# Sketched attention and a squared-relu FFN on one core: a shorter prologue, and later batches computed feature-major

## Chip, cores and metric

One core of a Trainium2 chip. The metric is device microseconds (us) of one execution; lower is better. A run is about 1.8 us longer than the span of its profile. With one core, "slow" only marks a run more than 1.5% above the fastest of the same kernel. Ratios use fast runs alone; medians below are of all runs, and where slow runs weigh in them, the fast ones are given too.

## The reference

Four batches, four heads, 1088 tokens, head size 32; then an FFN over all 4352 tokens, 128 wide, 2048 hidden.

```python
def phi(x):                                   # r = 8, so 64 features
    a = np.einsum('rd,bhsd->bhsr', S1, x)
    b = np.einsum('rd,bhsd->bhsr', S2, x)
    return np.einsum('bhsi,bhsj->bhsij', a, b).reshape(*x.shape[:-1], r * r)
q_p, k_p = phi(q), phi(k)
kv  = np.einsum('bhsf,bhsd->bhfd', k_p, v)
z   = np.sum(k_p, axis=2)
num = np.einsum('bhsf,bhfd->bhsd', q_p, kv)
den = np.einsum('bhsf,bhf->bhs', q_p, z)[..., None] + 1e-06
x   = (num / den), heads side by side         # 4352 x 128
g   = np.maximum(x @ w_in, 0.0) ** 2
out = g @ w_out
```

## The kernel before

Every operation is a node of a graph with engines that may run it and a modelled duration; the kernel schedules the graph itself when it is built, by a tuned list of priorities, and emits the instructions in that order. Each engine then works in that fixed order. All four batches use one form of attention, and all loads of batch 0 are on SyncE's queue:

```python
# key sketch: 32 wide, 64 columns                                     L416
nc.tensor.matmul(o[32*g : 32*g+32, :, j-j0, :], kT[i][:, 32*c : 32*c+32],
                 SK.rearrange("p x h r -> p x (h r)"), ...)
# keys times values, with a column of ones for z: 64 wide, 33 columns  L448
nc.tensor.matmul(t[64*(h%2) : 64*(h%2)+64, 33*(h//2) : 33*(h//2)+33],
                 kp[i][:, j, h, :], vp[i][:, h, j, :], ...)
# query sketch, both repeats (ab = 0, 1)                               L495
for ab in range(2): ... nc.tensor.matmul(at(hb[x])[64*y : 64*y+64, c0 : c0+n], SR[32*h : 32*h+32, ab], rhs, ...)
# numerator and denominator, token-major: 32 wide, 66 columns          L539
nc.tensor.matmul(at(nb)[32*cc : 32*cc+32, col(x=x, pr=pr)], qp[i][:, pr, n0 : n0+32], kvz[i][xx%2][:, pr], ...)
# ... normalise on VectorE, transpose back by TensorE (L571), copy into xT, then FFN:
# h = x w_in (L598), r = relu(h) (L607), g = r*r (L614), o += g w_out (L621)
```

Dummy matmuls on zeros (L290) keep TensorE busy before there is work.

## Time and profile before

| | before |
|---|---|
| median of the runs at hand, us | 123.16 (121.44 to 125.42) |
| span of the profile, us | 120.9 |
| busy: PE, DVE, ACT, POOL, us | 107.3, 94.4, 82.0, 25.1 |
| first FFN matmul, last compute, us | 22.36, 116.4 |

The prediction below quotes the windows and the timeline. Two windows it doesn't quote are needed later. Columns: stretch, its length, busy time (and instruction count) of PE, weight loads, VectorE, ScalarE, GpSimd, then granted clock, DMA share, GB/s.

```profile
57.00:74.00 17.00, 16.23 (x345) 9.56 (x347) 14.44 (x30) 12.14 (x20) 0.00 (x0) 1.00 0.11 18
74.00:91.00 17.00, 16.62 (x248) 9.45 (x250) 14.09 (x24) 14.62 (x21) 0.00 (x0) 1.00 0.11 18
```

From 57 us on the DMA engines are nearly idle: all loads are done. The row of the clock that TensorE was granted, in tenths of full speed, shows one dip, after the 2.46 us stop at 16.4. The clock records of the trace have half speed there, so such a stretch is called a half clock below.

```profile
PEclk9999995899999999999999999999999999999999
```

### The profile page before, as it was taken

To read this page: it belongs to the slowest core of one execution; us is meant where nothing else is said; L and a number is where in the kernel's file an instruction comes from. 1 tells how busy PE (TensorE), PEld (TensorE's weight loads), DVE (VectorE), ACT (ScalarE), POOL (GpSimd) and SP (SyncE) were. 2 spreads that over 40 slices of the span, in tenths; PEclk is the share of its full clock that TensorE was granted. 3 is DMA by queue.
4 is the path that set the end of the run, shared out by engine and by line. 5 is a ranking of instruction groups with operands and counts; after the bars stand their busy time and mean duration, and the time that the engine had idled before them with its cause. 6 is when DMAs were issued, how large, how long until landed. Compare 5 with 4: busy or idle time off the path is not lost.

```text
span 120.9 us, 4244 instructions
## 1 busy us (share of the span) xinstructions
PE 107.3 (89%) x1804; PEld 62.6 (52%) x1826; DVE 94.4 (78%) x168; ACT 82.0 (68%) x117; POOL 25.1 (21%) x55
## 2 busy tenths in 40 slices
PE   6999946999998999999999899999999999989530
PEld 2346736455664656556455755664466454645320
DVE  2599442499999999999895899768799987778810
ACT  3153700599769773898679567898966899999300
POOL 5219573726994500000000000000000000000000
PEclk9999995899999999999999999999999999999999
DMA  3985999999972900220000140220001304113051
GB/s 100 253 195 66 173 260 247 185 206 224 316 172 37 253 8 5 43 44 5 0 5 0 24 69 4 45 47 0 0 10 28 54 3 70 22 27 60 3 102 31
DMA packets 22700, 10.26 MB, mean 85 GB/s; under 512 B 19040, under 2 KB 20840, under 8 KB 22680
## 3 DMA queue, kind: packets, MB, share of 16 engines
q0 software_dynamic: 2560, 6.07, 23.3%
q1 hardware_dynamic: 20048, 3.90, 16.3%
q8 instruction: 14, 0.23, 0.9%
q14 instruction: 6, 0.05, 0.1%
q10 hardware_dynamic: 72, 0.01, 0.0%
HBM read 8.80 MB, written 2.23 MB: 91 GB/s over the span
## 4 chain that ended last, share of the span: by engine, by line
PE 59%; DVE 14%; ACT 12%; issue 10%; DVEq 0%; ACTq 0%
PE o L621 15%; PE h L598 13%; ACT r L607 12%; PE h L539 7%; PE h L495 7%; PE o L290 7%; DVE g L614 6%; PE a L448 6%; DVE kp L431 2%; DVE qT L472 2%; PE a L416 2%; PE h L416 1%; DVE qp L514 1%; DVE kT L403 1%; DVE osb L628 1%
## 5 line engine op out<-in xcount | busy, mean ns | idle before, releaser
L607 ACT ACTIVATE r<-h 128x1024 bf16<-128x1024 f32 x67 | 64.1, 1051 | 9.5 <-PE h L598 6.5
L614 DVE TENSOR_TENSOR g<-r 128x1024 bf16<-128x1024 bf16 x68 | 45.2, 687 | 6.0 <-PE o L621 4.5
L621 PE MATMUL o<-g,w_out 128*128 128x512 bf16 (+1 forms) x133 | 36.8, 367 | 2.3 <-DVE osb L628 1.2
L598 PE MATMUL h<-xT,w_in 128*128 128x512 bf16 (+1 forms) x137 | 37.7, 368 | 1.2 <-ACT r L607 0.9
L598 PEld LDWEIGHTS <-w_in 128*128 128x128 bf16 x144 | 15.4, 114 | 15.5 <-issue 2.4
L621 PEld LDWEIGHTS <-w_out 128*128 128x128 bf16 x144 | 12.7, 97 | 14.0 <-issue 3.8
L508 ACT COPY A<-h 128x512 f32<-128x512 f32 (+1 forms) x20 | 9.8, 525 | 6.5 <-PE h L495 6.5
L539 PE MATMUL h<-kvz,qp 128*32 128x66 f32 x576 | 10.6, 228 | 2.8 <-issue 2.5
L514 DVE TENSOR_TENSOR qp<-h,A 128x512 f32<-128x512 f32 x16 | 10.4, 683 | 2.3 <-ACT A L508 2.2
L539 PEld LDWEIGHTS h<-kvz,qp 128*32 128x32 f32 x576 | 9.2, 114 | 5.6 <-issue 3.0
L495 PE MATMUL h<-qT,SR 32*64 32x256 f32 (+1 forms) x320 | 10.8, 355 | 0.0
L290 PE MATMUL o<-wz 128*128 128x512 bf16 x26 | 9.2, 483 | 1.7 <-DVE mk L261 1.2
L448 PEld LDWEIGHTS a<-vp,kp 128*64 128x64 f32 x288 | 9.0, 138 | 2.7 <-issue 2.6
L448 PE MATMUL a<-vp,kp 128*64 128x33 f32 x288 | 9.9, 224 | 0.3
L495 PEld LDWEIGHTS h<-qT,SR 32*64 32x64 f32 x320 | 6.0, 131 | 3.8 <-DVE qT L472 0.4
L372 POOL DMA_DIRECT2D vin<-in_v_dram x12 | 6.6, 555 | 5.4 <-DMA vin<-in_v_dram 1.8
L628 DVE STREAM_TRANSPOSE osb<-o 128x512 f32<-128x512 f32 (+1 forms) x9 | 6.1, 679 | 1.6 <-PE o L621 1.4
L431 DVE TENSOR_TENSOR kp<-a,ka 128x1024 f32<-128x1024 f32 (+1 forms) x5 | 6.6, 1325 | 0.3 <-ACT ka L423 0.3
L388 POOL COPY vp<-vin 128x512 f32<-128x512 f32 x7 | 5.5, 805 | 5.9 <-DMA vin<-in_v_dram 5.3
L290 PEld LDWEIGHTS <-wz 128*128 128x128 bf16 x30 | 3.1, 119 | 5.9 <-issue 3.9
L472 DVE STREAM_TRANSPOSE qT<-qin 128x512 f32<-128x512 f32 (+1 forms) x8 | 5.8, 735 | 0.3 <-DMA qin<-in_q_dram 0.3
L555 DVE TENSOR_TENSOR xs<-h,rec 128x512 bf16<-128x512 f32 x8 | 5.5, 692 | 0.3
(50 smaller groups left out, 62.1 us busy)
## 6 DMA issues: line engine op xcount, KB each, us to landing
kin<-in_k_dram POOLq DMA_DIRECT2D x3, 544.0 KB, 8.8
qin<-in_q_dram POOLq DMA_DIRECT2D x3, 544.0 KB, 6.9
vin<-in_v_dram POOLq DMA_DIRECT2D x12, 128.0 KB, 6.5
out_dram<-osb SPq DMA_DIRECT2D x20, 64.0 KB, 1.9
vin<-in_v_dram SPq DMA_DIRECT2D x8, 64.0 KB, 3.1
kin<-in_k_dram SPq DMA_DIRECT2D x1, 288.0 KB, 4.3
qin<-in_q_dram SPq DMA_DIRECT2D x1, 288.0 KB, 2.7
kin<-in_k_dram SPq DMA_DIRECT2D x1, 256.0 KB, 2.8
```

Source lines behind the costliest of these rows:

```text
L290: nc.tensor.matmul(tiles["o"][0][:, 0:512], wz[:, 0:128], wz, start=True, stop=True)
L431: nc.vector.tensor_tensor(out=kp[i][:, j0:j1].rearrange("p j h (x y) -> p (j h) x y", y=R), in0=bb[:, :, None, :].to_broadcast([128, m, R, ...
L448: nc.tensor.matmul(t[64 * (h % 2) : 64 * (h % 2) + 64, 33 * (h // 2) : 33 * (h // 2) + 33], kp[i][:, j, h, :], vp[i][:, h, j, :], start=(j ...
L472: nc.vector.transpose(qT[i][:, 32 * c0 : 32 * c1], qin[i][:, 32 * c0 : 32 * c1])
L495: nc.tensor.matmul(at(hb[x])[64 * y : 64 * y + 64, c0 : c0 + n], SR[32 * h : 32 * h + 32, ab].rearrange("p x y -> p (x y)"), rhs, start=Tr ...
L508: nc.scalar.copy(at(sA).rearrange("p r e s -> p r (e s)")[:, :, 0:n], src(ab=0))
L514: nc.vector.tensor_tensor(out=qp5[:, u, x], in0=src(ab=1).rearrange("p r (e s) -> p r e s", e=2), in1=at(sA), op=ALU.mult)
L539: nc.tensor.matmul(at(nb)[32 * cc : 32 * cc + 32, col(x=x, pr=pr)], qp[i][:, pr, n0 : n0 + 32], kvz[i][xx % 2][:, pr].rearrange("p y d -> ...
L598: nc.tensor.matmul(at(hb)[:, step * w : step * w + N], w_in[:, 512 * (ct // E) : 512 * (ct // E) + 512].rearrange("p (c e) -> p e c", e=E) ...
L607: nc.scalar.activation(o, view(at(hb)), ACTF.Relu)
L614: nc.vector.tensor_tensor(out=at(gb)[:, 0 : W * N], in0=r, in1=r, op=ALU.mult)
L621: nc.tensor.matmul(at(ob)[:, 0:N], w_out[:, ct, :], at(gb)[:, N * w : N * w + N], start=(ct == 0), stop=(ct == CT - 1))
```

## The change

Three intents. (1) A shorter prologue: k of batch 0 in four pieces over two queues, the two sketch matrices loaded once and spread over the partitions by a matmul, a first FFN tile of 256 tokens. (2) Batches 1 to 3 keep features on the partitions, which makes TensorE's matmuls wider and removes the transposes behind them. (3) The denominator goes into the first repeat of the query, and this has to be repeated over the features: by TensorE for batch 1, by SyncE's DMA queue for batches 2 and 3. The core of the diff (cuts marked; priorities and engine choices were tuned anew):

```diff
-        LQ = {"SP": (0.45, 3.4)} if b == 0 else {"POOL": (0.65, 3.4)}
+        SPQ, ACQ = {"SP": (0.43, 3.4)}, {"ACT": (0.43, 3.4)}
+            o_kh = [[add(f"ldk{b}.{c0}.{y}", ACQ if y else SPQ, ...) for y in range(2)] for c0, c1 in ((0, 16), (16, 34))]
...
+    o_SX = add("SX", {"PE": pe(0.12)}, lambda e: nc.tensor.matmul(
+        at(stb)[:, 0 : 2 * R], repm, ST[:, 0 : 2 * R], start=True, stop=True), ...)
...   # batches 1 to 3: keys times values, 32 wide, 64 columns (L779)
+                        nc.tensor.matmul(at(kvb)[32 * h : 32 * h + 32, 0:F], lhsT, kp[i][0:n, j, h], ...)
...   # z of the keys (L751) folded into two sketches A and U of the query (L810), 272 columns
+        o_Z = add(f"Z{b}", {"PE": pe(0.5)}, f_Z, o_ka, vt(4), alloc=[zb])
+        o_W = add(f"W{b}", {"PE": pe(0.2)}, f_W, [o_ZT] + o_S2B, vt(4.6), alloc=[wb_])
...   # Ad = A / denominator, then spread over the features
+        o_Ad = add(f"Ad{b}", {"DVE": ..., "POOL": ...}, ... out=Ad[i], in0=As[i], in1=Rt[i][:, 0:272], op=ALU.mult ...)
+        if b == 1:
+            ... nc.tensor.matmul(at(rb_[x])[...], EI[32 * g : 32 * g + 32, ...], Ad[i][32 * g : 32 * g + 32, :], ...)
+        for g in range(4 if b > 1 else 0):
+            for pr in range(2):
+                    nc.sync.dma_start(
+                        out=Ar[i][:, pr, 272 * g : 272 * g + 272],
+                        in_=Ad[i][32 * g + 16 * pr : 32 * g + 16 * pr + 16, None, :].to_broadcast([16, 8, 272]))
...   # one repeat left on TensorE (L876), product with the spread one on VectorE (L886)
+                        in1=Ar[i][:, :, n0 : n0 + 272], op=ALU.mult)
...
-    sizes = [512] * 8 + [256]
+    sizes = [256] + [512] * 7 + [256] * 2
```

In the new schedule, batch 3's k, q and v are loaded by GpSimd behind a gate: a one-column copy that waits for the transposed key-value product of batch 2.

## The prediction

> **What bounds the kernel now.** I read the page's busy shares first, then the slices, the windows by stage, the chain of waits in order of time, and last the groups for durations. The busy shares:
>
> ```profile
> PE 107.3 (89%) x1804; PEld 62.6 (52%) x1826; DVE 94.4 (78%) x168; ACT 82.0 (68%) x117; POOL 25.1 (21%) x55
> ```
>
> Three engines are near full, so one total doesn't decide. The windows (columns: stretch, length, PE, PEld, DVE, ACT, POOL busy with counts, clock, DMA share, GB/s) show the stages:
>
> ```profile
> 0.00:22.50 22.50, 18.04 (x397) 11.06 (x402) 12.08 (x29) 6.93 (x17) 11.65 (x32) 0.92 0.87 189
> 22.50:40.00 17.50, 17.04 (x298) 10.05 (x300) 16.41 (x24) 15.28 (x23) 12.52 (x24) 1.00 0.83 188
> 40.00:57.00 17.00, 16.17 (x346) 9.58 (x341) 16.86 (x29) 12.76 (x19) 0.94 (x2) 1.00 0.26 53
> 91.00:108.00 17.00, 16.57 (x159) 9.04 (x160) 14.33 (x26) 15.57 (x18) 0.00 (x0) 1.00 0.19 32
> ```
>
> The first 22.5 us are a prologue: attention of batch 0, with PE's "busy" padded by 26 recorded dummy matmuls. From 22.5 to 57 PE and DVE are both full (DVE 16.86 of 17); at the end PE and ACT are. The timeline of the prologue and of the tail gives the two edges:
>
> ```profile
> 18.87 1.42 PE L539 MATMUL h<-kvz,qp 128*32 128x66 f32 x41 [2.46 <-issue]
> 22.36 0.59 PE L598 MATMUL h<-xT,w_in 128*128 128x512 bf16 x2
> 113.98 1.91 PE L621 MATMUL o<-g,w_out 128*128 128x256 bf16 x16 [1.24 <-DVE osb L628]
> 115.93 0.45 DVE L628 STREAM_TRANSPOSE osb<-o 128x256 f32<-128x256 f32 x1 [1.43 <-PE o L621]
> ```
>
> The first FFN matmul starts at 22.36, after a 2.46 us hole in which PE waited for nothing visible; the last work ends at 116.4 and the span at 120.9, so 4.5 us are the last stores. The middle, 94 us, is what PE's queue makes of FFN plus three attention batches. Its costs, from the chain (two records are one fp32 matmul):
>
> ```profile
> 44.44 0.59 PE h L416 x32
> 46.51 1.30 PE h L539 x80
> 53.50 1.06 PE a L448 x32
> 54.56 1.05 PE h L495 x32
> ```
>
> One batch is key sketch L416 1.28 (x32 0.58, x40 0.70), keys times values L448 2.4 (1.06 and about 1.3), query sketch L495 2.5 (1.05 + 1.05 + 0.39), numerator L539 2.45 (1.30 + 1.14), transposes 0.6: **9.2 us**. The FFN is 256 matmuls of 512 columns at 0.215 (two take 0.43 in the chain) and 32 of half that, 58.5. From 22.4 on PE must do 58.5 + 27.6 + 0.3 = 86.4 in 93.6 us; 7.2 us are holes (tail, phase changes, waits). PE sets the end, with DVE close behind.
>
> **What the Trainium skill says.** (1) "TensorEngine Tiling (Array Packing)", Tiling Modes: weights 64 wide leave two independent column tiles, 32 wide four, and row tiling multiplies this. The trace agrees: L448 (64 wide, 33 columns) takes 1.06 us for 32 records, L416 (32 wide, 64 columns) 0.59. (2) "ScalarE: Activation LUTs", What ACT_TABLE_LOAD costs: 186 ns plus 0.833 ns per element, 93 ns overlapped back to back; for 1024 that is 1039 and 946, and the relu group shows 1051 each and 64.1/67 = 957 of busy time. (3) "VectorE: DVE Perf Modes", The perf-mode tier table: a bf16 two-input op in SBUF runs at 2x, any PSUM source at 1x. It agrees: g (1024 bf16) 687 ns, qp (512 from PSUM) 683. (4) "GPSIMD Engine Reference", Engine selection: a two-input elementwise op is about twice as slow there, and the SBUF interface is shared with VectorE. Here only copies ran on POOL: minimum 612, maximum 1081 ns for one form, and one g took 960 against a median of 686, so mutual slowing exists and is rare.
>
> ```profile
> L614 DVE TENSOR_TENSOR g<-r x68: 648/686/960, 24.0 to 113.9; 128x1024 bf16<-128x1024 bf16 x68
> L388 POOL COPY vp<-vin x7: 612/615/1081, 8.5 to 39.4; 128x512 f32<-128x512 f32 x7
> ```
>
> **The change, part by part.** Counts are from the order of the built kernel.
>
> *Prologue.* k comes in four pieces issued alternately by SP and ACT, all before q and v, the sketch matrices as 16 rows spread by one matmul. All of k (544 KB) is needed at once; at some 250 GB/s (slices 2 and 6 show 253 and 260) from 1.7 us it lands near 4.4. Then: key transposes 1.5 on DVE, to 6; key sketch to 7.3; constants, first q transpose and four key products on DVE (about 0.69 + 0.69 + 0.95 + 0.69), to 10.6; second q transpose 1.0 and two qp of 0.42, to 12.6; a two-block numerator 0.5, normalising 0.9, transposes and an xT copy 0.9, to 15.0. Batch 1's key sketch, 0.6, sits ahead of the first FFN matmul, and its k, queued on POOL behind the gate near 9.5, lands near 14. So the first FFN matmul comes at about **16**, 6.4 earlier. But it is a 256-token tile, and 3.3 us of batch 0's PE work (numerators 1.9, half a query sketch 1.05, transposes 0.4) now comes later. Net gain on PE 3 us.
>
> *Feature-major batches on PE.* Keys times values becomes 32 wide with 64 columns, L416's form: 72 records at 0.59/32 = 1.3 instead of 2.4. The query product needs only one sketch: 2 x 16 records x 272 columns at L495's 32 x 256/1.05 = 7.8 columns per ns, 1.1 instead of 2.5. The numerator gets 8 tiles, 1.1 instead of 2.45, with no transposes after it (-0.6). Added: A and U, 16 records x 272 at L539's 80 x 66/1.30 = 4.06 per ns, 1.1; nine Z matmuls, W and the kv transpose, about 1.0. With the key sketch 1.3: **6.9**. Batch 1 spreads Ad by 16 matmuls of one row group each, so two tiles side by side instead of eight: about 2.0, so 8.9. Saved: 2.3 + 2.3 + 0.3 = 5 us. More phases at the chain's 0.16 "issue" each give back about 1.
>
> *ACT.* Gone: 12 evictions of 512 (0.59) and 3 of 128, the kvz copies and more, about 5 us a batch; new copies 2.4 (4.5 in batch 1). That room takes 22 squares while 17 relus leave: sum by rows 85 us, against 82.
>
> *DVE.* Per batch key and query transposes 2.8, qp 4 x 0.72, the denominator chain (P, transpose, reduce, reciprocal, spread) 2.7, and one key product of 1.2 or 1.5 or none (three of six go to POOL at an estimated 2.8 us each, 4497 ns for 2048 scaled from the GPSIMD page). The FFN: 46 squares and 18 relus of 1.2 instead of 68 and 1. All rows by duration give 102 us, where the same sum for the old kernel gives 99.5 and its busy time is 94.4; so about **97 us busy**, 2.5 more than before, in a shorter span.
>
> *Spreads by DMA* (batches 2 and 3): 16 SP issues of 139 KB written; about 8 us from Ad to the last landing, in a DMA queue that is idle after 40 us (share 0.26 and less). Hidden if the order holds.
>
> *Sum, by PE:* from 16, FFN 58.5 + batches 22.7 - 0.6 (already done) + batch 0's rest 3.3 = 84; holes 7.2 + 1; last compute at 108.2; stores 3.7 (the last four split over two queues save two issues of 0.4): 112. *By DVE:* 97 less 10.5 done by 16 leaves 86.5; the old kernel kept DVE 82.3/93.6 = 88% busy after its start; at 91% the end is 16 + 95 + 3.7 = 114.7. Between them, a span of **112.8**; a run is 1.75 above its span (122.65 against 120.9): **114.5 us**.
>
> **Rivals.** (a) *DVE becomes the bound* and cannot be kept over 88%: 16 + 98 + 3.7, a run near 119.5. For: 16.86 of 17 busy now, POOL shares its interface. Against: the split of relus and squares moves between ACT and DVE. (b) *The prologue gains nothing*: all k at once, more constants, batch 1's k behind the gate, or another fetch hole like the 2.46 one leave the first FFN matmul at 20: about 118. (c) *The spread or denominator is late* (ten steps from Ad through SP to qp) and PE starves before batch 2 or 3: 2 to 4 us each, 117 to 121. (d) *Everything fits*, PE's holes shrink to 4: 110.
>
> **Range and chances.** Rivals (a) to (c) each cost 3 to 6 us and seldom together; (d) gains 4. So 109.5 to 119.5 holds 8 in 10. Faster by over 2% means under 120.7: 0.93. Within 2%: 0.06. Slower: 0.01.
>
> **What would show it.** First FFN matmul at 15 to 18; FFN counts unchanged in columns; num, kv and query rows on PE down by half per batch; DVE 95 to 99 us, over 93% busy from 25 to 80; ACT 84 to 88; no second table load; last compute to end under 4 us. I am wrong if the middle, from first FFN matmul to last transpose, is over 97 us (then look at DVE waits), or the prologue is over 19.

## The result, and the profile after

The kernel is correct. Four runs took 130.91, 132.67 (slow), 130.15 and 130.46 us (median 130.69) against 123.16 before. The ratio, the mean of one kernel's fast runs over that of the other's fast runs of the same rounds (so not quite the ratio of these medians), is 1.065, 95% interval 1.050 to 1.079. **Slower by 6.5%**, where 7% faster was predicted.

Busy times first, against the line of before that the prediction quotes:

```profile
PE 112.2 (87%) x1321; PEld 59.9 (46%) x1321; DVE 96.9 (75%) x167; ACT 86.9 (67%) x122; POOL 33.3 (26%) x68
```

DVE and ACT are where they were predicted (97 and 85). PE has 483 fewer records and yet is busy 4.9 us longer. Part of that is clock: there are now two dips.

```profile
PEclk9999999958999999999999995999999999999999
```

The same windows as before:

```profile
0.00:22.50 22.50, 18.58 (x338) 11.34 (x338) 14.80 (x42) 8.56 (x23) 15.48 (x45) 1.00 0.77 182
22.50:40.00 17.50, 15.36 (x205) 9.61 (x205) 11.71 (x23) 10.86 (x17) 1.32 (x3) 0.90 0.09 22
40.00:57.00 17.00, 16.69 (x201) 7.66 (x193) 14.00 (x21) 13.01 (x21) 6.75 (x9) 1.00 0.52 124
57.00:74.00 17.00, 15.35 (x187) 6.93 (x186) 13.58 (x21) 14.10 (x17) 6.25 (x11) 1.00 0.75 158
74.00:91.00 17.00, 14.25 (x110) 6.61 (x110) 12.37 (x20) 12.46 (x18) 3.50 (x2) 0.90 0.21 39
```

Two stages lose. From 22.5 to 40 DVE is busy 11.71 where it was 16.41. From 57 to 91 PE is idle about 4.4 us of 34, and the DMA share from 57 to 74 is 0.75 where it was 0.11: batch 3's loads now fall here. The timeline names the waits (columns: start, busy us, engine, line, operation, count, and in brackets the idle time before and what ended it):

```profile
14.54 0.69 PE L632 MATMUL h<-kvz,qp 128*64 128x66 f32 x16 [0.65 <-DVE kvz L558]
...
16.87 0.38 ACT L673 COPY xT<-a 128x256 bf16<-128x256 bf16 x1
...
19.21 0.63 PE L931 MATMUL h<-xT,w_in 128*128 128x256 bf16 x4
...
25.87 0.71 PE L751 MATMUL h<-kab 128*32 128x32 f32 x13 [2.13 <-issue]
...
70.68 1.25 DVE L701 STREAM_TRANSPOSE kT<-kin 128x1024 f32<-128x1024 f32 x1 [1.69 <-DMA kin<-in_k_dram]
...
71.98 0.69 PE L718 MATMUL a<-SK,kT 128*64 128x64 f32 x16 [1.30 <-DVE kT L701]
...
75.18 0.72 DVE L886 TENSOR_TENSOR qp<-h,Ar 128x544 f32<-128x544 f32 x1 [2.56 <-DMA Ar<-Ad]
...
75.96 0.59 PE L931 MATMUL h<-xT,w_in 128*128 128x512 bf16 x2 [2.31 <-DVE qp L886]
```

The first FFN matmul comes at 19.2, not 16. At 23.75 TensorE stops for 2.13 us without a visible releaser, and a half clock follows. At 70.7 TensorE waits 1.30 us behind a transpose that waits for batch 3's k. At 73 the query product of batch 2 waits for its spread, TensorE stands behind it in its order, and again a half clock follows. GpSimd's own timeline shows what else was under way then:

```profile
58.50 0.78 POOL L834 TENSOR_TENSOR Ad<-As,Rt 128x272 f32<-128x272 f32 x1 [7.23 <-DVE Rt L831]
...
63.19 0.57 POOL L684 DMA_DIRECT2D kin<-in_k_dram  x1
...
66.49 0.56 POOL L684 DMA_DIRECT2D qin<-in_q_dram  x1
```

Ad, the source of batch 2's eight spread transfers, is done at 59.3, so the transfers and the 1.67 MB of batch 3 (62.6 to 67.0) are in flight together. From issue to landing a spread transfer took (minimum, median, maximum):

```profile
DMA to landing us min/median/max: 4.1/6.8/9.9
```

To compare sums I took all TensorE matmul records of a trace and counted the time from each one's start to the next one's start, capped at its own duration, to its line; the uncapped rest is idle. FFN is entered as the predicted 272 x 0.215 = 58.5 us, attention and dummies as counted, and "rest" is what remains: idle time, changes between kinds of work, and what half clock adds to the FFN. In us:

| | predicted | before | after | tiny spreads (e2, wrong result) | best version (e11) |
|---|---|---|---|---|---|
| first FFN matmul | 16 | 22.4 | 19.2 | 18.7 | 18.9 |
| FFN | 58.5 | 58.5 | 58.5 | 58.5 | 58.5 |
| attention behind that point | 25.4 | 28.4 | 29.6 | 28.5 | 28.7 |
| dummies behind that point | 0 | 0.4 | 1.8 | 1.4 | 0 |
| rest | 8.2 | 6.7 | 16.5 | 6.9 | 8.6 |
| last compute | 108.2 | 116.4 | 125.6 | 114.0 | 114.7 |

Against before, the change gains 3.2 at the start and loses 1.2 in attention, 1.4 in dummies and 9.8 in the rest: 9.2 later at the last compute. Of the rest, TensorE's idle time is 4.1 before, 8.9 after and 1.5 in e2.

### The profile page after: what moved, and what is told of

Same layout as the page of the kernel before. It is cut to its first block, busy times and chain, and to the rows that moved or that the text cites. A ratio compares the mean times of both kernels' runs of the same rounds, so it can differ in the third digit from the quotient of the medians.

```text
span 129.1 us, 3311 instructions
## 1 busy us (share of the span) xinstructions
PE 112.2 (87%) x1321; PEld 59.9 (46%) x1321; DVE 96.9 (75%) x167; ACT 86.9 (67%) x122; POOL 33.3 (26%) x68
## 3 DMA queue, kind: packets, MB, share of 16 engines
q0 software_dynamic: 2752, 6.07, 19.4%
## 4 chain that ended last, share of the span: by engine, by line
PE 37%; DMA 23%; DVE 12%; issue 7%; ACT 7%; SPq 7%; POOL 4%; ACTq 0%; DVEq 0%; POOLq 0%
PE o L957 12%; PE h L931 12%; DMA Ar<-Ad 10%; DMA kin<-in_k_dram 9%; SPq L861 7%; ACT r L940 4%; DMA vtl<-in_v_dram 3%; DVE r L942 3%; DVE g L950 2%; PE h L900 2%; DVE qp L886 2%; PE h L718 2%; DVE kT L701 1%; POOL Ad L834 1%; PE o L358 1%
## 5 line engine op out<-in xcount | busy, mean ns | idle before, releaser
L940 ACT ACTIVATE r<-h 128x1024 bf16<-128x1024 f32 x50 | 48.9, 1025 | 13.1 <-PE h L931 12.7
L950 DVE TENSOR_TENSOR g<-r 128x1024 bf16<-128x1024 bf16 x46 | 29.8, 680 | 1.2 <-PE o L957 0.3
L931 PEld LDWEIGHTS <-w_in 128*128 128x128 bf16 x160 | 16.8, 116 | 16.8 <-issue 7.4
L948 ACT ACTIVATE g<-r 128x1024 bf16<-128x1024 bf16 x22 | 23.1, 1065 | 1.2 <-PE o L957 1.0
L942 DVE TENSOR_SCALAR r<-h 128x1024 bf16<-128x1024 f32 x18 | 21.9, 1214 | 2.2 <-PE h L931 1.8
L957 PEld LDWEIGHTS <-w_out 128*128 128x128 bf16 x160 | 15.1, 99 | 16.4 <-issue 6.1
L886 DVE TENSOR_TENSOR qp<-h,Ar 128x544 f32<-128x544 f32 x12 | 8.3, 714 | 5.3 <-DMA Ar<-Ad 4.6
L735 POOL TENSOR_TENSOR kp<-kab 128x1280 f32<-128x1280 f32 (+1 forms) x3 | 6.7, 2242 | 16.5 <-ACT kab L725 16.5
L701 DVE STREAM_TRANSPOSE kT<-kin 128x1024 f32<-128x1024 f32 x3 | 3.7, 1245 | 4.5 <-DMA kin<-in_k_dram 4.5
L910 ACT CAST xT<-h 128x544 bf16<-128x544 f32 x6 | 3.6, 619 | 4.2 <-PE h L900 4.2
L900 PE MATMUL h<-qp,kvF 64*32 64x272 f32 x96 | 3.9, 398 | 1.4 <-DVE qp L886 1.3
L876 PE MATMUL h<-qT,SR 32*64 32x272 f32 x96 | 4.3, 413 | 0.0
```

Source lines behind the costliest of these rows:

```text
L735: (nc.gpsimd if e == "POOL" else nc.vector).tensor_tensor(out=kp[i][:, j0:j1].rearrange("p j h (x y) -> p (j h) x y", y=R), in0=bb[:, :, N ...
L886: nc.vector.tensor_tensor(out=qp[i][:, :, n0 : n0 + 272], in0=at(hb[x]).rearrange("p (r s) -> p r s", r=2)[:, :, 0:272], in1=Ar[i][:, :, n ...
L900: nc.tensor.matmul(at(nb)[32 * h : 32 * h + 32, 512 * x : 512 * x + 272], kvF[i][64 * y : 64 * y + 64, 32 * h : 32 * h + 32], qp[i][64 * y ...
L931: nc.tensor.matmul(at(hb)[:, step * w : step * w + N], w_in[:, 512 * (ct // E) : 512 * (ct // E) + 512].rearrange("p (c e) -> p e c", e=E) ...
L940: nc.scalar.activation(o, view(at(hb)), ACTF.Relu)
L942: nc.vector.tensor_scalar_max(o, view(at(hb)), 0.0)
```

## The experiments

**Theory A (collision).** Batch 2's spread shares the DMA engines with batch 3's loads, lands late, starves TensorE and brings the half clock. **Theory B (prologue).** Batch 1's k waits on GpSimd behind other work, and TensorE's stop at 24 us follows. **Rival.** TensorE's own work is larger than predicted, and the waits cost little. The kernels keep the changed kernel's order except for the named moves, made on the finished list by this helper:

```python
def shift(names, after):          # move operations behind the last of `after`
    ops = [o for o in order if o.name in names]
    for o in ops: order.remove(o)
    k = max(i for i, o in enumerate(order) if o.name in after) + 1
    order[k:k] = ops
```

### First call: before 123.67 (7 runs)

**e1: batch 3's loads early.**

```diff
+    shift([f"ldv3.{g}" for g in range(4)] + ["ldk3", "ldq3", "ldw3.0", "ldw3.1"],
+          [f"ldv2.{g}" for g in range(4)] + ["ldk2", "ldq2", "ldw2.0", "ldw2.1"])
```

> The changed kernel with batch 3's k, q and v loads issued on POOL straight after batch 2's (about 45 to 49 us) instead of behind the gate at 62; every other engine's order is as in the changed kernel. Theory A, collision: the spreads of Ad in batch 2 land 16.8 us after Ad because 1.67 MB of batch 3's loads share the transfer engines at 62 to 76 us; then the last of the eight lands under 10 us after Ad, the 2.3 us wait of PE at 74 us and the half clock after it are gone, and the time falls by 5 to 8 us, to 123 to 126. Rival B, the spread itself (eight issues of 136 KB on one queue) is slow in any company: the last still lands 14 us or more after Ad, time falls by under 2 us. Rival C, the loss is in PE's phases and DVE's load, not in transfers: falls by under 1 us.

125.33 us (121.70, 125.10, 125.56, 126.68; the clocks in that order 0.994, 0.986, 0.981, 0.972): 5.4 under the changed kernel by medians. Only the first counts as fast, and the record gives no ratio; it is 8.8 under the mean of the changed kernel's fast runs. At like clocks the gap is 4.2 (126.68 against 130.91, both at 0.972) and 4.6 (125.56 against 130.15, both at 0.981). Four windows of the changed kernel, of which the third holds TensorE's wait:

```profile
62.00:67.00 5.00, 5.00 (x30) 2.21 (x36) 4.90 (x7) 5.00 (x6) 4.59 (x9) 1.00 0.90 148
67.00:73.00 6.00, 4.70 (x74) 2.02 (x71) 3.93 (x7) 3.36 (x5) 0.05 (x1) 1.00 1.01 256
73.00:76.00 3.00, 0.69 (x4) 0.25 (x3) 0.72 (x1) 1.11 (x2) 1.94 (x1) 1.00 0.87 197
76.00:80.00 4.00, 3.55 (x26) 1.77 (x27) 3.09 (x4) 2.05 (x2) 0.00 (x0) 0.71 0.10 16
```

The first three of these in e1:

```profile
62.00:67.00 5.00, 5.00 (x26) 2.26 (x25) 4.79 (x7) 4.97 (x7) 0.22 (x1) 1.00 0.84 104
67.00:73.00 6.00, 6.00 (x80) 2.48 (x79) 6.00 (x10) 4.77 (x6) 0.00 (x0) 1.00 0.66 122
73.00:76.00 3.00, 3.00 (x22) 1.46 (x24) 1.96 (x3) 2.73 (x4) 1.95 (x1) 1.00 0.28 47
```

And the landing of e1's spread transfers of batch 2:

```profile
DMA to landing us min/median/max: 3.9/4.5/5.0
```

With the loads out of the way the maximum falls from 9.9 to 5.0 and TensorE is busy through all of 62 to 76. SyncE's eight issues take as long as before (7.8 us in e1, 8.3 after), so it is the transfer and not the issue that the loads stretch. The last landing comes 11.3 us after Ad (61.0 to 72.3), not under 10 as expected, but nothing waits for it. The collision also works the other way: batch 3's k took 7.5 us beside the spread (63.2 to 70.7) and 4.5 us beside the tiny spreads of e2 (58.9 to 63.4), and neither e1 nor e2 has the 1.30 us wait of TensorE behind it.

**e2: tiny spreads (wrong result on purpose).** Each transfer moves 8 of 272 columns; the rest of Ar is zeroed once.

```diff
-                        out=Ar[i][:, pr, 272 * g : 272 * g + 272],
-                        in_=Ad[i][... , None, :].to_broadcast([16, 8, 272]))
+                        out=Ar[i][:, pr, 272 * g : 272 * g + 8],
+                        in_=Ad[i][... , None, 0:8].to_broadcast([16, 8, 8]))
```

> The changed kernel with its 16 spread transfers kept in number and place but each moving 8 of the 272 columns (a wrong result on purpose; the buffer is cleared once on POOL in an idle stretch). Theory A (collision) and B (spread slow itself) both expect the time to fall by 7 to 10 us, to 121 to 124: batch 2's qp no longer waits, and batch 3's qp comes some 4 us sooner. Rival C (PE phases, DVE load): falls by under 1 us. How much lower than the run with the early loads it is, is the spread's own share apart from the collision.

119.97 us; 119.32, 119.88 and 120.06 at clocks of 0.999 to 1.000, and one slow run of 124.38 at 0.984; ratio to before 0.969 (0.964 to 0.974). This is below the 121 to 124 expected. With the spread nearly free the new kernel is only 3% faster than the old one, where 7% was predicted. The profile also lacks the stop at 24 us, so the spread is not the only difference.

**e3: four GpSimd copies later.** The copies that build the matrix EI (1.7 us on GpSimd) stood ahead of batch 1's loads; here they follow all of them.

```diff
+    shift(["EI"], [f"ldv1.{g}" for g in range(4)] + ["ldk1", "ldq1", "ldw1.0", "ldw1.1",
+                   "w_out0", "w_out1", "w_out2", "w_in2"])
```

> The changed kernel with the four copies on POOL that build the repeat matrix (8.04 to 9.74 us, needed only at 39) moved behind batch 1's loads. Theory D, batch 1's k is late because POOL's gate and load issues stand behind those copies: first FFN matmul from 19.2 to about 17.6, and the time falls by 1 to 1.5 us. Rival: k's landing (6.8 us after issue) is set by the traffic of all the first loads, so the first FFN matmul moves under 0.5 us and the time under 0.5.

127.72 us (126.98 to 130.62), ratio 1.032 (1.025 to 1.038): 3.0 under the changed kernel. The first FFN matmul came at 18.5 instead of 19.2, so the earlier start explains at most a quarter of it. The stop (2.41 us here) and the wait for batch 2's spread (3.05 us) stayed. Batch 1's k landed at 13.6 instead of 17.2 and the stop came all the same, so the second half of theory B falls. But this profile is of the slow run, 130.62 at a clock of 0.971, only 0.3 from the changed kernel's profiled run at 0.972. The three fast runs had clocks of 0.982 to 0.986 and left no trace, so how much of the 3.0 is the copies and how much a half clock less is open.

**e5: the last 16 of 30 dummies removed.**

```diff
+    order = [o for o in order if not (o.name.startswith("warm") and int(o.name[4:]) >= 14)]
```

> The changed kernel without the last 16 of the 30 dummy matmuls (32 PE instructions fewer before 28 us). In both kernels PE stood still for over 2 us with nothing to wait for, after 347 and 349 recorded matmuls, at 16.4 and at 23.8 us. Theory E, the stop belongs to a place in PE's instruction stream (its next instructions arrive late while the transfer engines are full): it comes again after about 349 recorded matmuls, which are now the first tile's FFN matmuls behind the nine Z matmuls, not the fifth Z record. Rival F, it belongs to the operation or the moment: it stays at the Z matmuls or goes. Time: within 1.5 us of the changed kernel either way; a colder PE clock in the first 20 us could cost as much.

127.15 us (125.25 at clock 1.000, then 126.82, 127.47, 128.51 at 0.985, 0.973, 0.985); ratio 1.020 (1.010 to 1.030). That is 3.5 under the changed kernel, where 1.5 at most was expected; the profiled run has no half clock, and no run shows what the rest is. The stop is still there (1.91 us), and still behind 349 matmuls and 349 weight loads, though 16 dummies are gone: it stands at a place in TensorE's instruction stream, not at an operation. In the traces of before, after, e1, e3 and e5 the counts ahead of it are 347 to 349 and 349 to 350, at 16.4 to 23.9 us.

### What the trace says of the stop

The DMA view lists packets by kind, and one kind is "instruction". From 14 to 23 us of the changed kernel there is none (columns: queue, kind, packets, MB, share of the engines; q0 carries GpSimd's transfers, q1 SyncE's):

```profile
q0 software_dynamic: 1189, 1.95, 97.4%
```

The next one is found from 23.0 to 23.6, just as TensorE runs dry:

```profile
q0 software_dynamic: 62, 0.14, 83.4%
q8 instruction: 1, 0.02, 11.1%
```

In e2, without a stop, it came between 14 and 23 (at 17.9):

```profile
q0 software_dynamic: 1172, 1.92, 96.8%
q8 instruction: 1, 0.02, 0.8%
```

Each is 16 KB on queue q8. They start at 13.1 and 23.3 us in the changed kernel, 12.4 and 17.9 in e2; the second ends at 24.4 and 19.1. All 14 traces, later ones included, show one pattern. In the seven with a stop at this place (before, after, e1, e3 and e5, and shorter ones in e9 and e12), TensorE goes on 1.2 to 1.5 us after the second packet's end. In the other seven that packet has ended 1.5 to 5.2 us before TensorE gets there. So the stop fits a late fetch of instructions while loads fill the DMA engines. This is a match in time: no run moves that packet alone. The next call tries whether a gap in the loads frees it.

### Second call: before 123.87 (23 runs)

**e6: a gap ahead of the second group of loads.** The four copies stand between the gate and that group, which delays it by 1.7 us.

```diff
+    shift(["EI"], ["gate1"])
```

> Only the four copies that build the spread matrix on GpSimd (1.7 us) move: from ahead of batch 1's first loads to between the gate and the second group of loads, so that this group is issued some 1.5 to 2 us later than in the shifted kernel with copies last. Theory F (TensorE stops because the 16 KB packet with its next instructions waits behind load packets on the DMA engines: it lands at 23.3 us in the changed kernel, 10.2 after the one before it, but at 17.9, 5.5 after, in the run with tiny spreads, which had no stop): the packet lands by 19.5 us, no TensorE stop of 1 us or more near record 698, no half clock near 26, the last step of batch 2's attention (Ad) ends near 55 instead of 59, the run takes 124 to 126. Rival G (the stop comes with the place in the program, the packet is asked for only when TensorE gets there): the stop of about 2 us stays at the same count, and the run takes 127 to 128 as with the copies moved last.

127.36 us (126.59, 126.69, 128.04, 128.77); ratio 1.036 (1.023 to 1.049). The first half of theory F held in its profile: no stop, though the packet came at 21.9 to 23.1 and not by 19.5. The second half failed: the time is e3's. The profile shows the reason only in part: the first FFN matmul came at 19.8, and batch 2's query product still waited 3.2 us for its spread. What the stop alone is worth can't be read from this.

**e7: gap and early loads together.**

```diff
+    shift(["EI"], ["gate1"])
+    shift([batch 3's loads], [batch 2's loads])        # as in e1
```

> The move of the copies together with batch 3's loads issued early. If stop (2.1 us and a half clock after it) and collision (5 us) are the two losses and independent, they add: 120 to 122, with batch 2's first query product not waiting for its spread and batch 3's still waiting 1.5 to 2 us. If the time lost in the prologue is given back to another wait (DVE as the bound), no faster than the kernel with early loads alone, 124 to 126.

123.02 us (120.31 and 122.77 at clock 0.995, 123.26 and 124.51 at 0.986). By medians 2.3 under e1 alone and 4.3 under e6 alone; only 120.31 counts as fast, 1.4 under e1's one fast run. The median is a little over the 120 to 122 that adding the two would give. The profile has no stop and no wait of batch 2's product. One wait of 1.5 us remains, for batch 3's spread.

**e8: as e7, and half of the spread transfers issued by GpSimd.**

```diff
-                    nc.sync.dma_start(
+                    (nc.sync, nc.gpsimd)[pr].dma_start(
```

> As the one before, but every second spread transfer is issued by GpSimd's queue instead of SyncE's, so that eight issues of about 0.75 us each run on two engines. If the issue sets the landing (6 us of issue for batch 3), the last landing comes 2.5 to 3 us earlier, batch 3's wait of 1.5 to 2 us goes, and the run takes 118.5 to 120.5. If the DMA engines set it (eight transfers of 139 KB written), nothing changes against the one before.

122.90 us (20 runs); ratio to before 0.999 (0.994 to 1.004): the same. The issue was not what set the landing. The spread of batch 3 in e7, 78 to 89 us:

```profile
q1 hardware_dynamic: 1840, 1.20, 60.6%
...
Ar<-Ad SPq DMA_DIRECT2D x8, 136.0 KB, 3.6
```

and in e8, 80 to 91 us:

```profile
Ar<-Ad SPq DMA_DIRECT2D x4, 136.0 KB, 6.9
Ar<-Ad POOLq DMA_DIRECT2D x4, 136.0 KB, 5.7
```

Issued twice as fast, each takes nearly twice as long. From 81 to 85 us of e7 the DMA engines are 0.89 to 0.90 busy and move 172 to 175 GB/s, with nothing but the spread and some stores: eight spread transfers alone nearly fill them. So all land late together: the first half of the product, which e7 starts 5.6 us after the first issue (79.4 to 84.9), starts 8.1 us after it (81.0 to 89.2).

**e4b: all spreads on TensorE.** The two branches for batch 1 and for batches 2 and 3 become the first one for all, scheduled anew, with the gap.

```diff
-        if b == 1:
+        if b >= 1:
...
-        for g in range(4 if b > 1 else 0):
+        for g in range(0):
```

> All three batches spread on TensorE, none by DMA; the order is scheduled anew, with the copies moved as well. Adds 32 matmuls of 272 columns, about 2 us of TensorE and 2.5 us of ScalarE for each of batches 2 and 3, and takes away the whole wait for landings. By the collision theory it is about as fast as the kernel with early loads and moved copies plus 2 to 4 us: 122 to 126, and certainly faster than the changed kernel's 130.7. If TensorE's work and not the wait was the loss, it is slower than the changed kernel.

126.37 us (126.11 to 126.69); ratio 1.030 (1.022 to 1.038). 4.3 under the changed kernel, 3.4 over e7's median and 6.1 over its fast run: no wait for a landing is left, and TensorE's and ScalarE's added work eats what that gives. (Its order also differs elsewhere, so the 3.4 is not that work alone.)

### Third call: before 123.52 (11 runs)

**e9: as e7, without the last six dummies.** These stand behind the first FFN matmul.

```diff
+    order = [o for o in order if not (o.name.startswith("warm") and int(o.name[4:]) >= 24)]
```

> The kernel with moved copies and early loads (123.0) without its last six dummy matmuls, which stand behind the first FFN matmul and take 1.2 to 1.4 us of TensorE there. If TensorE's work sets the end and the dummies are no longer hidden in waits, 1.2 to 1.5 us go: 121.0 to 122.0 for its runs at a clock near 0.99. If they stand in waits for other engines anyway (then their time turns into idle time of TensorE), nothing changes: 122.5 to 123.5; or a half clock comes in the idle time and it is slower.

121.35 us (120.91 to 122.51, six runs, all at clocks of 0.998 to 1.000); ratio 0.987 (0.982 to 0.993). 1.7 under e7's median, but over e7's one fast run. Against e8, which was as fast as e7 and has 13 fast runs, the ratios differ by 1.2%, some 1.4 us, where the dummies take 1.2 us in e8's trace. No run of e9 shows a half clock. In its profile the fetch packet is late again (23.2 to 24.1) in spite of the gap, with a stop of 0.94 us. So the gap does not reliably free the fetch: the remedy of theory F falls.

**e10: as e9, with the first FFN matmuls ahead of batch 1's first key sketch.**

```diff
+    shift(["ksk1.0"], ["m1.0.0"])
```

> As the one before, and the first sixteenth of the FFN stands ahead of batch 1's first key sketch, which waits for batch 1's k to land (17.2 us in the changed kernel). The first FFN matmul then comes at 17.2 to 17.6 instead of 18.4 to 19.9, in the idle time of that wait. If TensorE's order sets the end, 0.5 to 0.7 us go against the one before: 120.5 to 121.5; if batch 1's key product on VectorE is what the first tiles wait for, nothing changes.

121.79 us (121.34 to 122.30); ratio 0.989 (0.984 to 0.994): no gain. The first FFN matmul came at 19.4, behind a 0.27 us wait for a VectorE product, not at 17.2 to 17.6. The wait for batch 1's k is not what holds the first tile alone.

### Fourth call: before 123.39 (7 runs)

**e11: as e9, with the copies where the change has them** (early loads, six dummies fewer, nothing else).

> The best version so far (121.35: copies moved, early loads, no late dummies) with the four copies put back ahead of batch 1's first loads. If moving the copies is worth what the move alone gave (about 3 us against the changed kernel), 123.5 to 125; if its gain was the TensorE stop that also comes with it in some runs (0.94 us in the best version's own trace), 121.5 to 123.

121.41 us (120.03, 121.28, 121.55, 123.72), ratio 0.979 (0.972 to 0.986). The same as e9, so moving the copies is worth nothing in this company, although it gave 3.0 alone.

**e12: as e9, with batch 3's loads where the change has them** (gap, six dummies fewer).

> The best version with batch 3's loads put back where the changed kernel has them. By the collision theory batch 2's spread is late again, TensorE starves for about 3 us and goes to half clock: 125 to 127. If the early loads helped only by chance of the half clock, 121 to 123.

126.65 us (125.88 to 127.40), ratio 1.027 (1.022 to 1.032): 5.3 over e9; all runs of both count as fast, though they are of two calls. The wait for batch 2's spread is back (2.46 us), landing up to 9.7 us after issue, against 4.9 in e9, and so is the one for batch 3's k (1.24 us of TensorE). A stop of 0.93 us came too, in spite of the gap. This and e1 are two measurements of the same cause with different surroundings.

The busy times of e11, with e9 the best correct version:

```profile
PE 105.4 (89%) x1298; PEld 58.0 (49%) x1315; DVE 96.4 (82%) x167; ACT 86.6 (73%) x122; POOL 33.4 (28%) x68
```

And the row of its granted clock:

```profile
PEclk9999999999999999999999999999999999999999
```

No half clock, and PE is busy 6.8 us less than after (some 17 of its matmul records are missing: 1298 beside 1315 weight loads). It beats before by about 2% (e9 by 1.3%; at a limit of 2% the record classes e9 as the same and e11 as unclear) and the changed kernel by 9 us (across calls), with six dummies less and eight loads issued earlier.

## Why the prediction was wrong

The prediction said 114.5, 119.5 at most; the time was 130.7. Both of its own signs of being wrong came: the prologue ended at 19.2 (over 19), and the middle took 106.4 us (over 97). By its steps:

- **Spreads by DMA: failed, the largest loss.** "in a DMA queue that is idle after 40 us (share 0.26 and less). Hidden if the order holds." The share was read from the old kernel. In the new one batch 3's loads are gated on batch 2 and issued at 62.6 to 67.0, straight behind Ad. Predicted about 8 us from Ad to the last landing; measured 16.8 (59.3 to 76.1) with the loads beside it, 11.3 with them out of the way (e1), 8.8 for batch 3. Moving the loads is worth about 5 us: 5.3 from e12 to e9, 4.2 to 4.6 from the changed kernel to e1 at like clocks. Part of this is the load of batch 3's k, which the spread slows in turn. "The Trainium skill", page "DMA: Bandwidth & Descriptors", section Queues, rings and completion order, says that each DMA engine takes turns between the queues it has work for, packet by packet; the trace agrees in kind: q0's loads and q1's spreads run side by side, and the spread's median landing goes from 4.5 to 6.8. Rival (c) named the wait ("2 to 4 us each"), but not its cause, and it left the clock out.
- **Half clock: not in the sum at all.** The prediction had seen a clock of 0.92 in the first window of before and did not use it. In the changed kernel's trace there are two periods at half clock of 3.41 us each, and TensorE is busy 3.7 us longer behind its first FFN matmul than in e2 at full clock (97.0 against 93.3). "The Trainium skill", page "TensorE: Matmul & The Clock Gate", section What's actually happening, gives a free-running window of 3413 ns and half rate after one idle window or more. The length agrees. The condition doesn't: stops shorter than a window were followed by it (2.13 us in after), and a longer one was not (2.96 us in e6). In these traces it is the idle time inside one window that tells them apart. The clock records give the windows' edges, 3.41 us apart, and the windows view of the profile the busy time between them. TensorE was idle 1.89 to 2.41 us in each of the six full-clock windows that a half clock follows (before 1, after 2, e1 1, e3 2), and 1.80 us at most in every other one of all 14 traces; the 2.96 us of e6 lay across two windows (1.80 and 1.50 us idle). No run was made to test this.
- **Prologue: half right.** The gain was 3.2 us, not 6.4: 19.2 against 16. Most of the loss is batch 0's own chain: its first tile of xT was ready at 17.25, where the sum had 15.0. The sum let the first numerator follow the query products at 12.6. It began at 14.54, behind a path that the sum leaves out: keys times values (10.84 to 13.1) and four copies of their product, which ScalarE and VectorE make in turn (13.24 to 14.40). All of k landed at 5.7, not 4.4. Batch 1's k was said to be issued near 9.5 and to land near 14; it was issued at 10.4 and landed at 17.18, and its transposes and key sketch follow to 19.2. But k is the smaller part: in e3 it landed at 13.6 and the first FFN matmul still came at 18.5, and put ahead of that sketch it came at 19.4 (e10). What a shorter chain of batch 0 would give was not tried.
- **TensorE's attention: right in kind, under-sized.** Predicted 6.9 us a batch; by the records of e2 it is 7.9: key sketch 1.4 (1.3 predicted), keys times values 1.4 (1.3), query sketch 1.3 (1.1), numerator 1.2 (1.1), A and U 1.1 (1.1), and Z, W and the key-value transpose 1.5 ("about 1.0"). Batch 1's spread is 2.3 (2.0). Together 3.1 us over the 25.4. The last group was not worked out from a row but guessed, and it is the worst. Batch 0's late work, 3.3 predicted, is 3.2.
- **Six dummies behind the first FFN matmul, 1.4 to 1.8 us: left out.** The order of the built kernel showed them. Removing them with the loads early gave about 1.4 (e8 to e9).
- **Holes of 8.2: right in sum once the collision is gone.** The rest is 6.9 in e2 and 8.6 in e11, 16.5 in the changed kernel. In part this is luck: only 1.5 of e2's 6.9 is idle time of TensorE, most of the remainder is FFN matmul time above the 58.5 (63.3 when counted as the attention is).
- **DVE 97, ACT 85: right** (96.9, 86.9), and neither became the bound: in e11 DVE is busy 96.4 of 118.2. Rival (a) falls. (A side reading was off: mutual slowing of GpSimd and VectorE is called rare, but three of before's seven copies of that form took 1034 to 1081 ns, each beside a square on VectorE.)
- **Rival (b): came in part.** The first FFN matmul at 19.2 is close to its 20, and another hole came (2.13 us), but behind that matmul, so it is not what delayed it. (b) was offered as an alternative to (c), "seldom together". Both came, and each brought a half clock.

Added up against the predicted last compute of 108.2: start 3.2, attention 4.2 (1.1 of it half clock), dummies 1.8, rest 8.3 give 125.7; measured 125.6.

What stays open: why the fetch packet is late in some runs (starting at 13.1, then 23.3) and not in others (12.4, then 17.9) with much the same loads; what the stop costs apart from the half clock; what a wait that lies across two windows does in a kernel built to test it; and why the copies' move, 3.0 us alone, gives nothing beside the other two.

## What to carry to other kernels

A DMA queue that is idle in the old profile is no promise for the new schedule: list what the change itself moves into the stretch in which a transfer must land, and ask how many GB/s the transfer takes when it has the engines to itself. A wait of 2 to 3 us on TensorE may cost its own length and again half a clock window (here half of 3.41 us), so a rival that makes TensorE starve has to be priced with both. When a sum is built on one engine's work, size every small matmul group from a row of its form, and look into the built order for work, such as dummies, that the diff does not add but moves behind the starting line.

## What the Trainium skill lacked or had wrong

- "TensorE: Matmul & The Clock Gate", What's actually happening: half clock came after stops shorter than its idle window of about 3.4 us (2.13, 2.41 and 2.63 us), and not after 2.96 us in e6. In these traces 1.89 us or more of idle time inside one window brought it, and 1.80 us or less did not. The window's length, 3.41 us, is as stated (e1's half clock lasted two of them, 6.83 us).
- "Runtime: NRT & Kernel Launch", Instruction fetch mechanics, has instructions fetched in 16 KiB blocks and calls the cost of crossing into the next one mostly hidden. Here it was not: seven of 14 traces show TensorE stopping for 0.93 to 2.63 us at the same place, about 698 records into its stream, when a 16 KB packet of kind "instruction" comes late among the loads.
- "DMA: Bandwidth & Descriptors" gives no figure that I found for a spread inside SBUF with a repeated source: here eight transfers (1088-byte rows, 16 rows repeated eight times) reached 172 to 175 GB/s at 0.9 of the engines.
- "GPSIMD Engine Reference", Elementwise — side-by-side cycle accounting: the prediction's estimate from its 4497 ns, 2.8 us for a key product, of 1280 elements, is high: 2.39 us in the changed kernel, and 1.94 for 1024. (The shared interface that the prediction cites from Engine selection stands under Specifications of that page.)
